# First weight quarter's blocks one slot earlier, values' turn behind the normalisation, fewer filling products

## Chip, cores and metric

The kernel runs on one core of one Trainium2 chip. The metric is the device time of one execution in microseconds (us); a lower time is better. Each time below is that of the one core.

## What is computed

Three layers follow each other on a batch of 4 sequences with 576 positions and 512 channels. The change lies in the first: attention of 8 heads of 64 channels with a decay, while the weights of the second layer are made ready beside it.

```
scores = (q @ k.T) / sqrt(64) + cum[i] - cum[j]      # cum = cumsum(log(clip(f)))
attn   = softmax(where(j > i, -1e9, scores));  x = attn @ v          # 32 heads
u      = x + (x.T @ U @ V).T;  y = u + relu(u @ w_ch1) @ w_ch2       # 512 -> 2048 -> 512
out    = top-2 gated mixture of 4 single-head attentions over y
```

## The kernel before

**Stages.** Attention of the 32 heads comes first, two heads (a pair) per 128 partitions. Then a dense stage works off the rest of the second layer, and the mixture ends the program. Products of the second layer (hidden groups L704 and output groups L720) already run between the heads from head 10 on; they need the first quarter of the weights (`w1h`, `w1l`, `w2h`, `w2l`).

**The order.** Within the head stage the program writes down events: `put(h, us, do)` places a step at `us` in slot h (8.4 nominal units per slot, L1026). The events are sorted by that number, and each engine, SP's DMA queue included, gets its instructions in that order and works them off in order. The numbers set the order alone; how long a slot takes is decided by the engines. A slot runs below from the first score product of head h (PE, L285) to that of the next.

**A head's way.** PE multiplies scores in two parts (L285, tile `sc`), ScalarE takes exponentials (L305, L1050), and splits them into a high part (L310) and DVE's remainder (L313, tile `ph`). In the next slot PE weights the values (L341 to L345, or L357 for the odd heads of the first five pairs, which use the plain 32-bit form in two pieces; tile `av`), and DVE makes denominators (`den`, L403 or L405), their reciprocals (L408) and the normalised output (L422). Two slots ahead of a head PE makes the products for its row maxima (`ua` L201, `ub` L219), DVE takes the maxima (L206, L227, tile `mx`), PE turns them (`mt` L233), ScalarE makes a row of them (`mr` L239), and SP moves it to its place (L243). The `sc`, `ua` and `ub` tiles share two buffers.

**Values' turn.** From the second pair on, the largest value of a pair is found in an even slot: DVE takes the maximum per partition (`am` L363), PE turns it (`amt` L368, `value_turn`), and `value_power` makes a power of two of it in three small DVE operations (L375 to L377). At the start of the next odd slot PE spreads it (`rsp` L383), right behind `mt` and ahead of the second score part.

**Blocks.** The first quarter of the weights comes in 8 blocks of 128 x 512, as 64-bit words: SP reads (`raw`, L457 or L460), ScalarE narrows in two operations (`low_bits`, L442 and L443), DVE joins in two (`join_bits`, L449 and L450), ScalarE copies the high part and DVE subtracts the remainder (the last lines of `weight_events`, L1318 and L1320). `raw` and the joined block have two buffers each. The second quarter's blocks pass through the same function later, in slots of even number.

**Ones.** `busy` lets PE multiply a tile of ones with itself, a few products of 128 columns, whose result nobody reads.

**Sums.** In odd slots PE also makes the sums of the pair before (`gp` L943, `up` L960 and L962), ScalarE and DVE their parts (`g` L947 and L950, `ustage` L967). GpSimd subtracts 64 x 576 pieces of the next pair's q and k (L932), and from head 10 on masks the exponentials (L1056).

The events that the change touches, in the code before:

```
        put(h, 4.54, step, "amt", "am", value_turn)
        put(h, 5.6, step, "full", "amt", value_power)
        put(h + 1, 0.57, step, "rp", "full", value_spread)
        ...
        put(h - 1, 2.9, read)
        put(h, 8.0 if h % 2 else 6.1, bits)
        put(h + 1, 2.0, lambda: join_bits(st["to"], pairs_of_words(st["raw"])))
```

Of the kernel before, what the change touches and what calls it, by code (L numbers as in the profile page):

```python
# [15 lines left out]
OP = mybir.AluOpType  # L16
# [15 lines left out]
FT = FF // P // NQ  # L32
# [46 lines left out]
def f32(ap):  # L79
    return ap.bitcast(F32)  # L80
# [3 lines left out]
def kernel(  # L84
# [13 lines left out]
    nc = tc.nc  # L98
# [262 lines left out]
    def value_max(vr):  # L361
        am = small.tile([P, 1], F32, name="am")
        nc.vector.tensor_reduce(am[:], vr, AX.XYZ, OP.max, apply_absolute_value=True)  # L363
        return am
# [21 lines left out]
    def value_factor(rp):  # L386
        rs = small.tile([P, 1], F32, name="rs")
        nc.vector.reciprocal(rs[:], rp[:])
        return rs

    def value_high(vr, rs, vh):
        nc.scalar.mul(vh[:, :, :, 0:64], vr, rs[:, 0:1])

    def value_low(vr, rs, vh, vl):
        nc.vector.scalar_tensor_tensor(vl[:], vr, rs[:, 0:1], vh[:, :, :, 0:64], OP.mult,
                                       OP.subtract)
# [41 lines left out]
    def low_bits(wt, raw):  # L438

        lo, hi = raw[:, :, 0], raw[:, :, 1]  # L440
        byte = raw.bitcast(U8)[:, :, 3]
        nc.scalar.activation(wt.bitcast(I32), byte, AF.Copy, bias=-31.0 / 64.0, scale=1.0 / 32.0)  # L442
        nc.scalar.activation(f32(lo), f32(hi), AF.Copy, scale=2.0 ** -112)  # L443

    def join_bits(wt, raw):

        lo, hi = raw[:, :, 0], raw[:, :, 1]
        wi = wt.bitcast(I32)
        nc.vector.scalar_tensor_tensor(wi, lo, 3, wi, OP.logical_shift_left, OP.bitwise_or)  # L449
        nc.vector.scalar_tensor_tensor(wi, hi, -2147483648, wi, OP.bitwise_and, OP.bitwise_or)  # L450

    def read_block(q, t, from_=None):

        c0 = (q * FT + t % FT) * P
        raw = (from_ or stage).tile([P, 2 * DM], I32, name="raw", tag="wraw")
        if t < FT:
            nc.sync.dma_start(raw[:].rearrange("p (k n) -> p k n", k=KT),  # L457
                              w1[:, 2 * c0:2 * c0 + 2 * P].rearrange("(k p) n -> p k n", p=P))
        else:
            nc.sync.dma_start(raw[:], w2[c0:c0 + P, :])  # L460
        return raw

    def pairs_of_words(raw):
        return raw[:].rearrange("p (n two) -> p n two", two=2)
# [273 lines left out]
    dense, casts, sums, jobs, deferred, late = [], [], {}, [], [], []  # L738
# [287 lines left out]
    def put(h, us, do, *what):  # L1026
        events.append((h * SLOT + us, len(events), do, what))

    def early(us, do, *what):
        put(0, us - FIRST, do, *what)  # L1030
# [94 lines left out]
    def value_events(p):  # L1125

        h = 2 * (p - 1)
        st = {}

        def step(name, of, do):  # L1130
            st[name] = do(st[of]) if of else do(places[p % 2][1])

        def factor():
            st_rs[p] = value_factor(st["rp"])

        vr = places[p % 2][1]
        vh, vl = vhs[p % 2]
        if p < NPLAIN:
            vr = vr[:, 0:1]
            vh, vl = firsts[p % 2]  # L1140
        elif p < NPLAIN + 2:
            put(h + 1, 6.0, lambda: nc.vector.memset(vh[:, :, :, 64:65], 1.0))
        if p == 0:
            early(6.6, step, "am", None, lambda _: value_max(vr))
            put(0, 0.3, step, "amt", "am", value_turn)
            put(0, 0.35, step, "full", "amt", value_power)
            put(0, 2.05, step, "rp", "full", value_spread)
            put(0, 2.1, factor)
            put(0, 4.95, lambda: value_high(vr, st_rs[p], vh))
            put(0, 8.0, lambda: value_low(vr, st_rs[p], vh, vl))  # L1150
            return
        put(h, 1.95, step, "am", None, lambda _: value_max(vr))
        put(h, 4.54, step, "amt", "am", value_turn)
        put(h, 5.6, step, "full", "amt", value_power)
        put(h + 1, 0.57, step, "rp", "full", value_spread)
        put(h + 1, 2.2, factor)
        put(h + 1, 6.1, lambda: value_high(vr, st_rs[p], vh))
        put(h + 2, 1.9, lambda: value_low(vr, st_rs[p], vh, vl))
# [132 lines left out]
    def weight_events(q, t, h):  # L1291

        w1h, w1l, w2h, w2l = W[0]
        st = {}

        def read():
            st["raw"] = read_block(q, t)

        def bits():
            if q == 0:  # L1300
                st["to"] = stage.tile([P, DM], F32, name="wst", tag="wst")[:]
            else:
                st["to"] = w32[q][:, t, :]
            low_bits(st["to"], pairs_of_words(st["raw"]))

        put(h - 1, 2.9, read)
        put(h, 8.0 if h % 2 else 6.1, bits)
        put(h + 1, 2.0, lambda: join_bits(st["to"], pairs_of_words(st["raw"])))
        if q:
            return  # L1310
        cs = slice(t * P, t * P + P)
        dh, dl = (w1h[:, :, cs], w1l[:, :, cs]) if t < FT else (w2h[:, t - FT, :],
                                                               w2l[:, t - FT, :])

        def view():
            return st["to"].rearrange("p (k n) -> p k n", k=KT) if t < FT else st["to"]

        put(h + 1, 6.7, lambda: nc.scalar.copy(dh, view()))  # L1318
        put(*((h + 2, 2.3) if t < 2 * FT - 1 else (h + 1, 8.38)),
            lambda: nc.vector.tensor_tensor(dl, view(), f32(dh), OP.subtract))  # L1320

    def largest_event(t, h):

        def largest_of():
            if t == 0:
                largest[1] = small.tile([P, 2, FT], F32, name="wam0", bufs=1)
            nc.vector.tensor_reduce(largest[1][:, t // FT, t % FT:t % FT + 1], w32[1][:, t, :],
                                    AX.X, OP.max, apply_absolute_value=True)

        put(h, 2.45, largest_of)  # L1330
# [26 lines left out]
        for _ in range(n):  # L1357
            nc.tensor.matmul(some[:, 0:P], every[:], every[:], start=True, stop=True)

    for h in range(10):  # L1360
        put(h, 0.54, busy, 8 if h < 3 else 4)
        if h < 3 or h % 2:
            put(h, 2.1, busy, 14 if h < 3 else 10)
    early(12.35, busy, 24)

    NHEAD = 2 * NPAIR
# [5 lines left out]
    for p in range(NPAIR):  # L1372
        value_events(p)
        split_events(p)
        mix_events(p)
        for n, (j, us, ta, td) in enumerate(((0, 2.1, 3.95, 5.45), (1, 2.1, 3.95, 5.45),
                                             (0, 5.9, 7.6, 8.2), (1, 7.1, 8.75, 10.3))):
            if n < PER_PAIR[p]:
                fill_events(2 * p + j, us, ta, td)
    for t in range(2 * FT):  # L1380
        weight_events(0, t, (4, 5, 6, 7, 8, 9, 10, 11)[t])
        weight_events(1, t, 2 * (t + 7))
        largest_event(t, (20, 22, 24, 26, 28, 29, 30, 31)[t])
    put(9, 8.35, ffn_prepare, 0)
# [745 lines left out]
```

## Time and profile before

| what | value |
|---|---|
| median of 3 runs (lowest to highest) | 786.92 us (786.47 to 787.28) |
| the profiled execution's own time | 787.25 us |
| its span, first to last instruction | 785.5 us |
| busy: PE, DVE, ACT, POOL | 752.3, 598.5, 436.1, 201.9 us |
| head stage (slots 0 to 31) | 16.8 to 266 us of the span |
| slots 3 to 9, mean of one | 7.34 us |
| slots 10 to 29, mean of one | 8.51 us |

The span is what the profile shows of that execution; the 1.7 us beside it lie before its first and behind its last instruction. In the profile, PE is TensorE's matmuls, PEld its weight loads, DVE VectorE, ACT ScalarE, POOL GpSimd, SPq the DMA queue of SyncE. L12 is line 12 of the kernel. Matmuls overlap each other, so their starts tell more than their durations. In brackets stands how long the engine was idle before an instruction, and what ended that wait.

### The profile page before, as it was taken

To read this page: it belongs to the slowest core of one execution; us is meant where nothing else is said; L and a number is where in the kernel's file an instruction comes from. 1 tells how busy PE (TensorE), PEld (TensorE's weight loads), DVE (VectorE), ACT (ScalarE), POOL (GpSimd) and SP (SyncE) were. 2 spreads that over 40 slices of the span, in tenths; PEclk is the share of its full clock that TensorE was granted. 3 is DMA by queue.
4 is the path that set the end of the run, shared out by engine and by line. 5 is a ranking of instruction groups with operands and counts; after the bars stand their busy time and mean duration, and the time that the engine had idled before them with its cause. 6 is when DMAs were issued, how large, how long until landed. Compare 5 with 4: busy or idle time off the path is not lost.

```text
span 785.5 us, 19296 instructions
## 1 busy us (share of the span) xinstructions
PE 752.3 (96%) x7399; PEld 649.0 (83%) x7399; DVE 598.5 (76%) x1659; ACT 436.1 (56%) x893; POOL 201.9 (26%) x357
## 2 busy tenths in 40 slices
PE   4899999999999999999999999999999999999996
PEld 4799888989998999877777777777778888878873
DVE  6889999999999959988773685366644688887763
ACT  6778887877786725644421242113312366776673
POOL 8734466665564200000020000000000611111110
PEclk9999999999999999999999999999999999999999
DMA  5668665566563165844133224300103475344322
GB/s 163 174 195 227 194 179 169 178 183 180 172 188 116 61 197 184 266 145 168 54 99 109 73 80 158 113 1 1 62 31 76 120 182 139 76 118 97 91 75 95
DMA packets 65708, 101.97 MB, mean 130 GB/s; under 512 B 8864, under 2 KB 43664, under 8 KB 65616
## 3 DMA queue, kind: packets, MB, share of 16 engines
q1 hardware_dynamic: 65248, 100.09, 43.0%
q8 instruction: 58, 0.95, 0.5%
q10 hardware_dynamic: 368, 0.66, 0.3%
q14 instruction: 34, 0.28, 0.1%
HBM read 53.25 MB, written 23.74 MB: 98 GB/s over the span
## 4 chain that ended last, share of the span: by engine, by line
PE 53%; DVE 2%; ACT 1%; issue 0%; DMA 0%; ACTq 0%; DVEq 0%
PE cps L720 17%; PE hps L704 16%; PE pq L1636 6%; PE pv L1680 3%; PE sc L285 3%; PE po L1732 2%; PE ub L219 1%; PE av L341 1%; PE av L345 1%; PE av L343 1%; PE pos L1732 1%; PE ua L201 0%; DVE ph L313 0%; ACT pf L305 0%; DMA out_dram<-ost 0%
## 5 line engine op out<-in xcount | busy, mean ns | idle before, releaser
L709 ACT ACTIVATE hh<-hps 128x288 f16<-128x288 f32 (+1 forms) x128 | 52.4, 410 | 210.6 <-PE hps L704 186.1
L710 DVE SCALAR_TENSOR_TENSOR hl<-hps,hh 128x288 f16<-128x288 f32 (+1 forms) x128 | 58.2, 454 | 79.5 <-ACT hh L709 79.1
L227 DVE CUSTOM_DVE_ANT_0 ub<-ub,maskm 128x448 f32<-128x448 f32 x192 | 82.4, 429 | 2.3 <-PE ub L219 0.7
L285 PE MATMUL sc<-qa,ka 128*128 128x288 f32 (+4 forms) x288 | 72.0, 309 | 1.6 <-DMA qa<-mr 1.1
L726 DVE SCALAR_TENSOR_TENSOR yc<-cps,back,yc 128x288 f32<-128x288 f32 x96 | 49.3, 514 | 24.5 <-PE cps L720 23.0
L285 PE MATMUL sc<-qb,kb 128*128 128x288 f32 (+4 forms) x288 | 63.5, 302 | 0.0
L341 PEld LDWEIGHTS <-ph 128*128 128x128 f16 x645 | 58.9, 97 | 1.2 <-DVE o L422 0.6
L345 PEld LDWEIGHTS <-ph 128*128 128x128 f16 x645 | 59.3, 97 | 0.4 <-DVE ph L313 0.4
L343 PEld LDWEIGHTS <-ph 128*128 128x128 f16 x645 | 59.3, 98 | 0.3
L1863 POOL TENSOR_SCALAR_AFFINE_SELECT pf<-pf 128x128 f32<-128x128 f32 (+1 forms) x80 | 23.9, 318 | 116.3 <-ACT pf L305 115.6
L285 PEld LDWEIGHTS sc<-qb,kb 128*128 128x128 f32 x288 | 52.3, 189 | 1.5
L206 DVE CUSTOM_DVE_ANT_0 ua<-ua,maskm 128x576 f32<-128x576 f32 x48 | 36.5, 761 | 21.0 <-PE ua L201 12.3
L313 DVE TENSOR_TENSOR ph<-pf,ph 128x512 f16<-128x512 f32 (+1 forms) x66 | 47.6, 734 | 6.4 <-ACT ph L310 6.4
L285 PEld LDWEIGHTS sc<-qa,ka 128*128 128x128 f32 x288 | 48.8, 189 | 3.7 <-issue 1.2
L313 DVE TENSOR_TENSOR ph<-aside,ph 128x512 f16<-128x512 f32 (+1 forms) x63 | 49.8, 802 | 1.2 <-ACT ph L310 1.0
L1056 POOL TENSOR_SCALAR_AFFINE_SELECT aside<-aside 128x128 f32<-128x128 f32 (+1 forms) x80 | 39.6, 514 | 38.5 <-ACT aside L305 29.9
L305 ACT ACTIVATE aside<-sc 128x512 f32<-128x512 f32 (+1 forms) x63 | 38.7, 617 | 18.3 <-PE sc L285 16.5
L720 PE MATMUL cps<-hh,w16b 128*128 128x288 f16 x256 | 48.3, 286 | 0.3 <-DVE hl L710 0.3
L720 PE MATMUL cps<-hh,w1lf 128*128 128x288 f16 x256 | 48.4, 286 | 0.0
L720 PE MATMUL cps<-hh,w16a 128*128 128x288 f16 x256 | 48.4, 286 | 0.0
L305 ACT ACTIVATE pf<-sc 128x512 f32<-128x512 f32 (+1 forms) x66 | 39.7, 609 | 13.1 <-PE sc L285 9.4
L720 PEld LDWEIGHTS <-w16b 128*128 128x128 f16 x384 | 37.4, 98 | 10.2 <-issue 0.8
(281 smaller groups left out, 2464.4 us busy)
## 6 DMA issues: line engine op xcount, KB each, us to landing
raw<-in_w_dram SPq DMA_DIRECT2D x32, 512.0 KB
ust<-udram SPq DMA_DIRECT2D x13, 576.0 KB
ydram<-yc SPq DMA_DIRECT2D x10, 576.0 KB
aside<-in_qk_dram SPq DMA_DIRECT2D x8, 576.0 KB
room<-in_qk_dram SPq DMA_DIRECT2D x8, 576.0 KB
udram<-ustage SPq DMA_DIRECT2D x16, 288.0 KB
ydram<-ust SPq DMA_DIRECT2D x8, 576.0 KB
yc<-ydram SPq DMA_DIRECT2D x8, 576.0 KB
```

The source lines that it names most:

```text
L227: nc.vector.tensor_tensor_reduce(ub[:, bk, off:off + w], ub[:, bk, off:off + w], maskm[:, S - w:S], 1.0, NEG, OP.add, OP.max, mx[:, t:t + 1])
L285: nc.tensor.matmul(ps[:, bk, off:off + w], wa, xa, start=bk not in banks[:n], stop=bk not in banks[n + 1:])
L305: nc.scalar.activation(pf[:, 0:S].rearrange("p (c n) -> p c n", c=2) if whole else pf[:, 0:n], view, AF.Exp, scale=ISC)
L313: nc.vector.tensor_tensor(pl[:, o0:o0 + n], pf[:, 0:n], ph[:, o0:o0 + n], OP.subtract)
L341: nc.tensor.matmul(av[:, it, :], ph[:, c:c + P], vh[:, jt, :], start=first, stop=False)
L343: nc.tensor.matmul(av[:, it, 0:64], ph[:, c:c + P], vl[:, jt, :], start=False, stop=False)
L345: nc.tensor.matmul(av[:, it, :], pl[:, c:c + P], vh[:, jt, :], start=False, stop=last)
L704: nc.tensor.matmul(ph[:], wa[:, k, fs], xa[:, k], start=n == 0, stop=n == 3 * KT - 1)
L709: after(lambda: nc.scalar.activation(hh[:], ph[:], AF.Relu), lambda: nc.vector.scalar_tensor_tensor(hl[:], ph[:], 0.0, high, OP.max, OP.su ...
L710: lambda: nc.vector.scalar_tensor_tensor(hl[:], ph[:], 0.0, high, OP.max, OP.subtract))
L720: nc.tensor.matmul(pc[:], wa[:, t, dsl], xa[:], start=n == 0, stop=n == 3 * FT - 1)
L726: nc.vector.scalar_tensor_tensor(yc[:, d, :], pc[:], back, yc[:, d, :], OP.mult, OP.add)
```

## The change

It edits numbers of the order, and leaves out products; nothing else of the computation is touched.

- The values' turn comes after the attention product, and `value_power` after the normalisation (all pairs from the second on).
- The eight blocks of the first quarter are taken one slot earlier. Those whose number of slot is odd (four of them) are narrowed behind the next slot's exponentials, joined behind its normalisation, and their high part is made in the slot after. Their reads but the first stand behind the moves of the even slot before. The last block's remainder takes the usual place.
- The ones from slot 3 on are left out: 4 products in each of slots 3 to 9, and 10 more in 3, 5, 7 and 9.

```diff
-        put(h, 4.54, step, "amt", "am", value_turn)
-        put(h, 5.6, step, "full", "amt", value_power)
+        put(h, 4.7, step, "amt", "am", value_turn)
+        put(h, 6.57, step, "full", "amt", value_power)
...
-        put(h - 1, 2.9, read)
-        put(h, 8.0 if h % 2 else 6.1, bits)
-        put(h + 1, 2.0, lambda: join_bits(st["to"], pairs_of_words(st["raw"])))
+        late = h % 2
+        put(h - 1, 6.65 if late and t else 2.9, read)
+        put(*((h + 1, 3.2) if late else (h, 6.1)), bits)
+        put(h + 1, 6.6 if late else 2.0,
+            lambda: join_bits(st["to"], pairs_of_words(st["raw"])))
...
-        put(h + 1, 6.7, lambda: nc.scalar.copy(dh, view()))
-        put(*((h + 2, 2.3) if t < 2 * FT - 1 else (h + 1, 8.38)),
-            lambda: nc.vector.tensor_tensor(dl, view(), f32(dh), OP.subtract))
+        put(*((h + 2, 1.4) if late else (h + 1, 6.7)), lambda: nc.scalar.copy(dh, view()))
+        put(h + 2, 2.3, lambda: nc.vector.tensor_tensor(dl, view(), f32(dh), OP.subtract))
...
-    for h in range(10):
-        put(h, 0.54, busy, 8 if h < 3 else 4)
-        if h < 3 or h % 2:
-            put(h, 2.1, busy, 14 if h < 3 else 10)
+    for h in range(3):
+        put(h, 0.54, busy, 8)
+        put(h, 2.1, busy, 14)
...
-        weight_events(0, t, (4, 5, 6, 7, 8, 9, 10, 11)[t])
+        weight_events(0, t, (3, 4, 5, 6, 7, 8, 9, 10)[t])
```

DVE at the end of slot 4, from the second of the row maxima (ISA with `ub`; the second ISA row of each reads the result) to the denominators. Before:

```order
L227 ISA ub,mx_96<-ub,maskm 128x448
L227 ISA mx_96 128x1
L375 TENSOR_REDUCE ar_82<-amt 1x1
L376 TENSOR_SCALAR ar_82<-ar_82 1x1
L377 TENSOR_SCALAR ar_82<-ar_82 1x1
L227 ISA ub,mx_96<-ub,maskm 128x320
L227 ISA mx_96 128x1
L403 TENSOR_SCALAR den<-av 128x5
```

And with the change, up to the same place:

```order
L227 ISA ub,mx_96<-ub,maskm 128x448
L227 ISA mx_96 128x1
L227 ISA ub,mx_96<-ub,maskm 128x320
L227 ISA mx_96 128x1
L403 TENSOR_SCALAR den<-av 128x5
```

The three operations on `ar` have left the row of maxima. DVE a little later, at the start of slot 5, from the normalisation to the next head's first maximum. Before:

```order
L422 TENSOR_TENSOR room<-av,rn 128x5x64
L313 TENSOR_TENSOR ph_144<-pf,ph_144 128x512
L313 TENSOR_TENSOR ph_144<-aside,ph_144 128x512
L449 SCALAR_TENSOR_TENSOR wst<-raw,wst 128x512
L450 SCALAR_TENSOR_TENSOR wst<-raw,wst 128x512
L388 RECIPROCAL rs<-rsp 128x1
L206 ISA ua,mx_90<-ua,maskm 128x2x288
```

With the change, from the normalisation to the remainder ahead of that maximum:

```order
L422 TENSOR_TENSOR room<-av,rn 128x5x64
L375 TENSOR_REDUCE ar_82<-amt 1x1
L376 TENSOR_SCALAR ar_82<-ar_82 1x1
L377 TENSOR_SCALAR ar_82<-ar_82 1x1
L449 SCALAR_TENSOR_TENSOR wst<-raw,wst 128x512
L450 SCALAR_TENSOR_TENSOR wst<-raw,wst 128x512
L313 TENSOR_TENSOR ph_144<-pf,ph_144 128x512
L313 TENSOR_TENSOR ph_144<-aside,ph_144 128x512
L449 SCALAR_TENSOR_TENSOR wst<-raw,wst 128x512
L450 SCALAR_TENSOR_TENSOR wst<-raw,wst 128x512
L388 RECIPROCAL rs<-rsp 128x1
L1321 TENSOR_TENSOR w1l<-wst,w1h 128x4x128
```

The three operations come behind the normalisation here, followed by a second join and, later, by a block's remainder. PE at the end of slot 4, as a difference, from the last products for the maxima to the next head's scores:

```order
 L219 MATMUL ub<-ka_128,qa_126 128x192
 L219 MATMUL ub<-ka_128,qa_126 128x64
+L357 MATMUL av<-vw_158,ph_146 128x65 x9
 L368 MATMUL amt<-ident,am 1x128
-L357 MATMUL av<-vw_158,ph_146 128x65 x9
 L285 MATMUL sc<-qa_138,ka_140 128x288
 L285 MATMUL sc<-qb_139,kb_141 128x288
```

The values' turn has moved from ahead of the attention product's second piece to behind it.

## Rows read from the trace of the kernel before

**Rows 1.** The page's slices of the span: PE's busy tenths, its granted clock.

```profile
PE   4899999999999999999999999999999999999996
PEclk9999999999999999999999999999999999999999
```

**Rows 2.** Slot 5: us; busy PE, PEld, DVE, ACT, POOL (xinstructions); clock, DMA, GB/s.

```profile
53.27:60.62 7.35, 7.31 (x104) 6.98 (x103) 6.50 (x22) 5.36 (x11) 3.42 (x4) 1.00 0.69 198
```

**Rows 3.** Timeline of DVE, slots 4 and 5: start us, us, engine line operation out<-in.

```profile
52.19 0.27 DVE L375 TENSOR_REDUCE ar<-amt 1x1 f32<-1x128 f32 x1
...
52.75 0.48 DVE L227 CUSTOM_DVE_ANT_0 ub<-ub,maskm 128x320 f32<-128x320 f32 x1
...
53.50 0.16 DVE L403 TENSOR_SCALAR den<-av 128x5 f32<-128x5 f32 x1 [0.22 <-PE av L357]
...
56.15 0.68 DVE L449 SCALAR_TENSOR_TENSOR wst<-raw,wst 128x512 int32<-128x512 int32 x1
...
57.47 0.16 DVE L388 RECIPROCAL rs<-rsp 128x1 f32<-128x1 f32 x1
...
58.14 0.77 DVE L206 CUSTOM_DVE_ANT_0 ua<-ua,maskm 128x576 f32<-128x576 f32 x1 [0.51 <-ACT g L947]
```

**Rows 4.** Timelines of PE and DVE, slots 6, 7, 10 and 11.

```profile
65.60 0.76 PE L219 MATMUL ub<-ka,qa 127*128 127x448 f32 x4 [0.94 <-ACT pf L305]
...
66.31 2.12 PE L357 MATMUL av<-vw,ph 128*128 128x65 f32 x18
...
68.47 0.17 DVE L403 TENSOR_SCALAR den<-av 128x5 f32<-128x5 f32 x1
...
68.92 0.39 PE L1358 MATMUL some<-every 128*128 128x128 bf16 x4
...
70.85 0.72 PE L1358 MATMUL some<-every 128*128 128x128 bf16 x10
...
97.02 2.12 PE L357 MATMUL av<-vw,ph 128*128 128x65 f32 x18
...
99.55 0.15 DVE L403 TENSOR_SCALAR den<-av 128x5 f32<-128x5 f32 x1
...
101.33 0.46 DVE L710 SCALAR_TENSOR_TENSOR hl<-hps,hh 128x288 fp32r<-128x288 f32 x1 [0.53 <-ACT hh L709]
```

**Rows 5.** Timelines of GpSimd and DVE, slots 7 and 10.

```profile
68.77 1.42 POOL L932 TENSOR_TENSOR kb<-room,ka 64x576 fp32r<-64x576 f32 x1
...
69.55 1.18 DVE L313 TENSOR_TENSOR ph<-aside,ph 128x512 f16<-128x512 f32 x1
...
94.93 0.69 DVE L450 SCALAR_TENSOR_TENSOR wst<-raw,wst 128x512 int32<-128x512 int32 x1
...
95.00 1.47 POOL L1056 TENSOR_SCALAR_AFFINE_SELECT pf<-pf 128x128 f32<-128x128 f32 x2
...
95.54 0.78 DVE L1320 TENSOR_TENSOR w2l<-wst,w2h 128x512 fp32r<-128x512 f32 x1
```

**Rows 6.** Timeline of DVE, slot 13.

```profile
119.77 0.68 DVE L1320 TENSOR_TENSOR w2l<-wst,w2h 128x512 fp32r<-128x512 f32 x1
...
120.37 0.68 DVE L313 TENSOR_TENSOR ph<-aside,ph 128x512 f16<-128x512 f32 x1
...
123.73 0.77 DVE L206 CUSTOM_DVE_ANT_0 ua<-ua,maskm 128x576 f32<-128x576 f32 x1 [1.06 <-PE ua L201]
```

**Rows 7.** Waits of DVE from 125 to 262 us; then the timeline of slot 17.

```profile
DVE ua L206 <- PE ua L201: 3.1, 7, 0.6
...
150.41 0.48 DVE L422 TENSOR_TENSOR room<-av,rn 128x320 f32<-128x320 f32 x1
...
150.60 0.08 PEld L233 LDWEIGHTS mt<-ident,mx 128*5 128x5 f32 x1 [0.34 <-DVE mx L227]
...
150.71 0.17 PE L383 MATMUL rsp<-ar,every 128*128 128x1 bf16 x1
...
155.11 0.77 DVE L206 CUSTOM_DVE_ANT_0 ua<-ua,maskm 128x576 f32<-128x576 f32 x1 [0.48 <-PE ua L201]
```

## Prediction

> **What bounds the kernel now.** I read the page's slices first: PE is the busy engine nearly everywhere, and its granted clock is at full speed in every slice, also in the first, where PE works less than half of the time [rows 1]. The change touches the stretch of 32 attention heads, from 17 to 266 us, one slot per head. So I then cut that stretch into slots (a slot runs from the first score product of a head to that of the next) and read the busy time by slot, the waits, and the order of time on each engine. In slot 5 DVE works 6.50 of 7.35 us [rows 2]; from slot 6 to 12 it pauses nearly nowhere, and the waits that I found in slots 5 to 13 are short: 0.22 us for a finished attention product before its denominators and 0.51 before the first maximum in slot 5 [rows 3], 0.53 for a hidden part in slot 11 [rows 4], 1.06 before the first maximum in slot 13 [rows 6]. So DVE sets the pace of slots 5 to 12, in step with PE: once in each slot DVE needs PE's products for the maxima (ua) and once or twice PE waits for DVE. Later, in the odd slots, a short chain is what ends last: DVE's last maximum, PE's turn of the maxima (mt), the spread of the value factor (rsp), the second score products, a hidden or output group, the sums (gp), ua, and DVE again. DVE waits for ua in 7 slots of that stretch, 3.1 us in all [rows 7].
>
> **Values' turn behind the normalisation.** The three small operations of value_power take 0.56 us from start to start (52.19 to 52.75, where the next maximum starts) [rows 3]. They now stand behind the last maximum and the normalisation. So mt may start 0.56 us sooner, but rsp comes right behind mt on PE and needs the third of the three, and the second score products queue behind rsp. Maxima and normalisation move up by 0.56 and the three take the place behind them, so that they end where the normalisation ended. In slot 17 that is 150.41 + 0.48 = 150.89; with 0.04 from one engine to the next (68.43 to 68.47, worked out below), rsp starts at 150.93 instead of 150.71 [rows 7]: 0.22 us later. There DVE already waits 0.48 us for ua, and that wait grows. This holds in the odd slots in which PE waits for the maxima before mt: 13, 15, 17, 19, 23, 27 and 29, while in 21 and 25 PE comes late by itself. The term is 7 x 0.22 = **+1.5 us**. Its ends: nothing, if something that I don't see takes up the 0.22, and 7 x 0.56 = 3.9.
>
> In slots 3, 5, 7 and 9 the delay is larger, about 0.7 us, since DVE there waits for the attention product before it can go on (0.22 us in slot 5 [rows 3]), and the three operations no longer fill that wait. But there the 14 ones go from PE's odd slots, 4 of them ahead of mt and 10 ahead of gp; four take 0.39 and ten 0.72 us [rows 4], so each holds PE for 0.33 / 6 = 0.055, the four for 0.22 and the ten for 0.55, and the second pays for most of the delay. All 68 of them (4 in each of seven slots, 10 in four) are worth nothing beyond that, as PE then only waits longer for DVE's maxima.
>
> **Blocks one slot up.** A block costs DVE a join (two operations, 56.15 to 57.47 where the next one starts, so 1.32 us [rows 3]) and a remainder (119.77 to 120.37, where the 0.68 of the row are overlapped by the next, so 0.60 [rows 6]). The sum over all eight blocks stays. What moves is one block's 1.92 us, out of slots 12 and 13 and into slot 5 (the join of the first block is put at the end of slot 4 and done at the start of slot 5). In slot 5 it fills the wait of 0.51 us; at the end only the join's 1.32 comes back, because the last remainder (119.77) lies in front of the 1.06 us for which DVE waits anyway [rows 6]. So 1.92 - 0.51 - 1.32 = **+0.1 us**.
>
> **Joins in pairs.** The blocks of odd slots are now joined behind the normalisation, so DVE has two joins in each of slots 5, 7, 9 and 11, and none in 6, 8 and 10. In an even slot DVE thus reaches the denominators 1.32 + 0.56 = 1.88 us sooner. It then waits for PE, which reaches the end of the attention product sooner by less: in slot 6 by 0.94, the wait of ub for ScalarE's exponentials that the later narrowing removes, 0.22 for the ones and 0.11 for the values' turn that now stands behind the product. In the profile both arrive together (66.31 + 2.12 = 68.43 and 68.47 [rows 4]), so at the start of slot 7 DVE newly waits 1.88 - 1.27 = 0.6. Slots 8 and 9 have the same pattern: 0.6. In slot 4 nothing of this is gained except the 0.56 that no longer fills the wait, less 0.11: 0.45. In slot 10 PE has a hidden group and no ones, and gains the 0.11 alone; DVE came 0.41 after the product (97.02 + 2.12 = 99.14 and 99.55 [rows 4]), so it waits 1.88 - 0.41 - 0.11 = 1.36, of which the 0.53 that it now waits for the hidden part is to be taken off, since the join covers that: 0.85. Together 0.45 + 0.6 + 0.6 + 0.85 = **+2.5 us**; the ends are 0 (PE runs ahead enough) and 3.0 (the join covers nothing). In the following odd slots the time isn't won back, since there DVE, with two joins, is the one that PE waits for.
>
> **Beside GpSimd.** The first remainder of the exponentials takes 1.18 us in slot 7 while GpSimd's subtraction runs (68.77 to 70.19), and 0.68 alone [rows 5, 6]. The first now comes 2 us later, behind the first join, when that subtraction has ended: up to -0.5 in each of slots 5, 7 and 9; I take -0.4, because the subtraction comes later too and may still reach into it. In its place the join stands beside GpSimd, and a weight's remainder beside GpSimd's next subtraction. The nearest rows, beside its selection: a join's second half takes its usual 0.69, a weight's remainder 0.78 instead of 0.68 [rows 5, 6]. By these: -1.2 + 3 x 0.1 = **-0.9 us**, with ends of -1.5 and +1.5. The Trainium skill's GPSIMD Engine Reference (section 8, Key points) speaks against that: GpSimd shares its SBUF interfaces with VectorE, and contends with instructions that have two SBUF inputs. The join has two such inputs; by that rule it would stretch as the remainder did, and this term would be 0 and the time 0.9 us longer. The rows show no join beside a GpSimd subtraction, so the run will tell.
>
> **Other edits.** Narrowing behind the exponentials and the high part behind its join cost ScalarE the same work as before; ScalarE isn't what paces these slots, so 0. The reads of the odd slots' blocks move past the moves on SP's queue, and each now waits there for a join that DVE does early in the next slot, with the next row of maxima (qa<-mr) queued behind it. That row is needed at the start of the slot after. DVE's join stands in the first half of its slot, so the row leaves before the slot ends: 0. If it came late in slots 6, 8 and 10, PE would wait by what is missing, a few tenths each.
>
> **Sum.** +1.5 + 0.1 + 2.5 - 0.9 = +3.2 us on the profiled execution's 787.25 us, so 790.45. That execution lies 0.33 above the median of 786.92; against the median I forecast 786.92 + 3.2 = **790.1 us**, slower by 0.4%.
>
> **Rivals.** (1) *PE runs ahead, faster.* If the exponentials' 0.94 and the ones bring the attention product to its end before DVE asks for it, the paired joins cost nothing, and what DVE waited goes: 0.51 and 0.22 in slot 5, 0.53 in slot 11 and, with a join less in slot 12 and PE no longer late, 0.66 of slot 13's 1.06. That is 1.9 off the median: 785.0. For it speaks that PE is gated by ScalarE in slots 6, 8 and 12; against it, that PE gains 1.27 where DVE gains 1.88. It decides at a wait before the denominators in slots 7 and 9 under 0.1 us. (2) *The two halves partly cancel.* The paired joins cost half as much and the late chain half, 1.25 + 0.75 - 0.9 + 0.1 = 1.2: 788.1, within what can be told from no change. (3) *TensorE's clock falls.* Without the ones PE pauses longer from slot 3 on. The clock stayed full in a slice with PE busy under a half [rows 1], so I hold this unlikely; if one slot ran at 1.2 GHz, its 7.31 us of PE work [rows 2] would take twice as long, 786.92 + 3.2 + 7.3: 797. The Trainium skill (TensorE: Matmul & The Clock Gate, Part 1) says that the throttled clock is the default and activity releases it, which is what the ones would serve; no row here shows the clock at the lower level.
>
> **Chances.** Forecast 0.58, rival 1 0.18, rival 2 0.20, rival 3 0.04. About 0.2%, 1.57 us, is what can be told from no change. Rival 1 is the faster case, 0.18; rival 2 the same, with 0.04 of the forecast's own low end: 0.24; slower 0.58. The forecast's own range is 788.5 to 791.9; with the greater part of rival 1, the range for 8 in 10 is 785.0 to 791.9.
>
> **What would show it.** Right: in slots 7 and 9 DVE's den waits some 0.6 us for av; two joins stand in slots 5, 7, 9 and 11; rsp waits for ar and the wait of DVE for ua in slots 15, 17, 19, 23 and 27 is about 0.7 instead of 0.5; slot 16 starts about 2 us later than before. Wrong: no wait at den, slot 14 starts no later than before, or the granted clock below 1.00 in a slice.

## The result and the profile after

The changed kernel takes 797.46 us (median of 4 runs, 795.54 to 799.49) where the kernel before takes 787.10 beside it: 1.0124 times as long, 95% interval 1.0105 to 1.0142, or 10.4 us slower. The forecast was 790.1 us and its range ended at 791.9. Run a second time it took 795.63 us (4 runs, 794.91 to 796.68), 1.0107 times before (1.0090 to 1.0124). The profiled execution took 798.38 us, its span 796.7 against 785.5.

By the starts of the slots, the profiled execution is 3.15 us behind before at slot 4, 8.0 at slot 13 and 10.3 at slot 30. The second run's profile, which lacks the first loss, is 0.2 us ahead at slot 4, 4.7 behind at slot 13 and 8.6 at slot 30. Slot 27 is 2.43 us longer there and 0.86 in the first profile, so 1.6 of the last belong to a stretch at the lower clock (0.5 from 245.7 to 249.1 us). Behind the head stage both profiles lose another 0.8 us, at 303 us of the kernel before: PE waits there 0.4 and 0.6 us for the factor of another spread (L490). No part alone shows this loss.

PE's share and its granted clock in 40 slices of the changed kernel's page, which answer to [rows 1]:

```profile
PE   4797899999999999999999999999999999999997
PEclk9899999999999999999999999999999999999999
```

The second slice is below full speed. In windows: us; busy PE, PEld, DVE, ACT, POOL (xinstructions); clock, DMA, GB/s. The first and second are the stretches at half the clock (1.2 GHz), the third and fourth are slots 5 and 6:

```profile
23.27:26.69 3.42, 3.34 (x18) 3.10 (x19) 3.25 (x13) 3.25 (x8) 3.27 (x3) 0.50 0.82 194
...
33.51:36.93 3.42, 3.42 (x20) 3.23 (x20) 2.21 (x5) 2.31 (x5) 0.24 (x1) 0.50 0.05 12
56.38:66.57 10.19, 7.32 (x90) 6.22 (x89) 9.79 (x29) 7.06 (x16) 5.95 (x4) 1.00 0.58 184
66.57:72.84 6.27, 6.27 (x56) 6.16 (x56) 5.72 (x18) 6.21 (x14) 0.15 (x1) 1.00 0.82 211
```

Slot 5 has grown from 7.35 [rows 2] to 10.19 us, slot 6 has shrunk from 7.62 to 6.27. DVE is busy for 9.79 of the 10.19. Slots 7 and 9 are like slot 5, slot 8 like slot 6. The timeline of slot 5 (start, us, engine, line; in brackets the wait and what ended it), and then of slot 17, which answers to [rows 7]:

```profile
56.55 0.17 DVE L403 TENSOR_SCALAR den<-av 128x5 f32<-128x5 f32 x1 [0.65 <-PE av L357]
...
58.07 1.42 POOL L932 TENSOR_TENSOR kb<-aside,ka 64x576 fp32r<-64x576 f32 x1
...
58.22 1.82 DVE L449 SCALAR_TENSOR_TENSOR wst<-raw,wst 128x512 int32<-128x512 int32 x1
60.08 0.69 DVE L450 SCALAR_TENSOR_TENSOR wst<-raw,wst 128x512 int32<-128x512 int32 x1
...
60.80 0.62 ACT L1320 CAST w1h<-wst 128x512 fp32r<-128x512 f32 x1 [1.77 <-DVE wst L450]
...
62.46 0.76 PE L219 MATMUL ub<-ka,qa 127*128 127x448 f32 x4 [1.21 <-ACT ph L1050]
...
63.30 0.67 DVE L1321 TENSOR_TENSOR w1l<-wst,w1h 128x512 fp32r<-128x512 f32 x1
63.37 1.87 POOL L932 TENSOR_TENSOR qb<-aside,qb 64x576 fp32r<-64x576 f32 x1 [3.88 <-ACT qb L886]
63.88 0.76 DVE L206 CUSTOM_DVE_ANT_0 ua<-ua,maskm 128x576 f32<-128x576 f32 x1
...
156.88 0.13 DVE L227 DVE_READ_ACCUMULATOR2_ANT mx<- 128x1 f32 x1
157.05 0.50 DVE L227 CUSTOM_DVE_ANT_0 ub<-ub,maskm 128x320 f32<-128x320 f32 x1
157.46 0.22 DVE L405 TENSOR_SCALAR den<-av,rs 128x5 f32<-128x5 f32 x1
...
158.47 0.27 PE L233 MATMUL mt<-ident,mx 128*5 128x128 f32 x1
158.65 0.27 DVE L375 TENSOR_REDUCE ar<-amt 1x1 f32<-1x128 f32 x1
159.13 0.14 DVE L377 TENSOR_SCALAR ar<-ar 1x1 int32<-1x1 int32 x1
159.32 0.16 PE L383 MATMUL rsp<-ar,every 128*128 128x1 bf16 x1 [0.58 <-DVE ar L377]
...
163.74 0.77 DVE L206 CUSTOM_DVE_ANT_0 ua<-ua,maskm 128x576 f32<-128x576 f32 x1 [0.75 <-PE ua L201]
```

Two things stand out. The first half of the join (L449) takes 1.82 us beside GpSimd's subtraction, not 0.68 [rows 3], and all that follows on DVE comes later; ScalarE's high part waits 1.77 us for it ahead of the exponentials, and PE's ub 1.21 us for these. And rsp waits 0.58 us for ar, where it came 0.11 behind mt before [rows 7]. Waits from 36 to 265 us, from within slot 2 to slot 29 (us in total, times, longest; the 2.7 of the first row stands in slot 2):

```profile
DVE ua L206 <- PE ua L201: 9.6, 11, 2.7
...
PE rsp L383 <- DVE ar L377: 6.6, 11, 0.6
...
DVE den L403 <- PE av L357: 2.1, 5, 0.6
```

The wait of rsp stands in 11 odd slots; that of DVE for the denominators in slots 3, 5, 7, 9 and 10.

### The profile page after: what moved, and what is told of

The parts are those of the page before. It is cut to its first block, busy times and chain, and to the rows that moved or that the text cites. A ratio compares the mean times of both kernels' runs of the same rounds, so it can differ in the third digit from the quotient of the medians.

```text
span 796.7 us, 19157 instructions
## 1 busy us (share of the span) xinstructions
PE 753.7 (95%) x7331; PEld 648.3 (81%) x7331; DVE 601.9 (76%) x1659; ACT 436.7 (55%) x893; POOL 199.3 (25%) x357
## 4 chain that ended last, share of the span: by engine, by line
PE 50%; DVE 3%; ACT 1%; DMA 1%; issue 0%; SPq 0%; ACTq 0%; DVEq 0%
PE cps L720 16%; PE hps L704 15%; PE pq L1636 6%; PE pv L1680 3%; PE sc L285 3%; PE po L1732 2%; PE ub L219 1%; PE av L341 1%; PE av L345 1%; PE av L343 1%; DMA ust<-udram 1%; PE pos L1732 1%; PE ua L201 0%; DVE ph L313 0%; DVE uam L576 0%
## 5 line engine op out<-in xcount | busy, mean ns | idle before, releaser
L206 DVE CUSTOM_DVE_ANT_0 ua<-ua,maskm 128x576 f32<-128x576 f32 x48 | 36.5, 761 | 24.4 <-PE ua L201 16.2
L313 DVE TENSOR_TENSOR ph<-pf,ph 128x512 f16<-128x512 f32 (+1 forms) x66 | 47.2, 728 | 6.4 <-ACT ph L310 6.4
L313 DVE TENSOR_TENSOR ph<-aside,ph 128x512 f16<-128x512 f32 (+1 forms) x63 | 47.3, 761 | 2.6 <-ACT ph L310 2.6
L1056 POOL TENSOR_SCALAR_AFFINE_SELECT aside<-aside 128x128 f32<-128x128 f32 (+1 forms) x80 | 37.3, 484 | 41.6 <-ACT aside L305 35.6
```

Of the source, the lines that this page charges most:

```text
L313: nc.vector.tensor_tensor(pl[:, o0:o0 + n], pf[:, 0:n], ph[:, o0:o0 + n], OP.subtract)
```

## Experiments

Each is compared with runs of the kernel before on the same chip, whose medians were 786.79 to 787.19 us.

### The three parts, each alone

**The turn.**

```diff
-        put(h, 4.54, step, "amt", "am", value_turn)
-        put(h, 5.6, step, "full", "amt", value_power)
+        put(h, 4.7, step, "amt", "am", value_turn)
+        put(h, 6.57, step, "full", "amt", value_power)
```

> The kernel before with the values' turn alone: amt behind the attention product, value_power behind the normalisation. Theory A (the three parts add up, and this one costs what the late odd slots show): in the trace of the changed kernel the denominators of slot 17 come 0.39 us sooner against the maxima, but rsp starts 1.86 us behind the denominators' start where it started 1.08 behind them before, so 0.39 us later in each of 7 late odd slots, and some 0.4 to 0.7 in slots 3, 5, 7 and 9: +2.7 + 2 = +4.5 us. Rival B (the turn costs little by itself, since in slots 3 to 9 the joins and not rsp end last): +2 us or less. If the turn is what brings TensorE's clock to its lower level in slots 1 and 2 as in the changed kernel's profile, this run shows it and a slot 3 that starts 3 us late; if not, slot 3 starts at most 0.3 us late.

Measured: 793.16 us, 1.0076 (1.0064 to 1.0088), +6.0. The profiled execution (792.34) loses 0.73, 0.71, 0.60 and 0.59 in slots 3, 5, 7 and 9, 2.6 together, and 2.95 from slot 13 to 30. Slot 1 ran at half the clock here too, yet slot 2 started no later. So A in kind: the median lies 1.5 us above its 4.5, the profiled execution 0.6. The loss before slot 4 is not the turn's.

**The ones.**

```diff
-    for h in range(10):
-        put(h, 0.54, busy, 8 if h < 3 else 4)
...
+    for h in range(3):
+        put(h, 0.54, busy, 8)
```

> The kernel before with the ones from slot 3 on left out, and nothing else. Theory A (the ones fill PE's pauses and cost nothing there; the clock stays full without them): within 0.5 us of before, -0.5 to +0.5, the granted clock 1.00 in all slices. Rival B (they keep the clock at full speed, or they hold PE up): B1, without them the clock falls in a stretch between slot 3 and 10, +2 us or more; B2, they hold up mt and gp, and the time falls by up to 7 x 0.22 + 4 x 0.55 = 3.7 us.

Measured: 786.66 us, 1.0000 (0.9989 to 1.0012). In the mean nothing, as A said, but both rivals hold in part, and they cancel. Slots 3 and 5 are 0.55 us shorter each, and slot 8 begins 1.37 us ahead of before. Then this profile shows the clock at half, from about 80 to past 86 us (same columns as the windows above), and slot 8 takes 9.55 instead of 7.63 us:

```profile
75.00:78.00 3.00, 3.00 (x29) 2.90 (x27) 2.89 (x7) 2.96 (x7) 0.00 (x0) 1.00 0.97 236
78.00:80.00 2.00, 0.93 (x6) 0.69 (x6) 1.97 (x4) 2.00 (x5) 0.00 (x0) 0.96 0.34 71
80.00:82.00 2.00, 2.00 (x12) 2.00 (x12) 1.93 (x9) 2.00 (x4) 0.99 (x1) 0.50 0.92 363
```

PE was busy for 0.93 of the 2 us ahead of it. Of 12 executions, four had a mean clock of 0.989 to 0.994 and took 788.0 to 789.8 us; the other eight had 0.996 or more and took 785.6 to 786.9. The 23 executions of before beside them all had 0.996 or more. The ones do not hold the clock in every execution, though: beside the other experiments 3 of 52 executions of before had 0.993 or 0.994, and two runs below that keep the ones have 0.988 or less throughout.

**The blocks.**

```diff
-        put(h, 8.0 if h % 2 else 6.1, bits)
-        put(h + 1, 2.0, lambda: join_bits(st["to"], pairs_of_words(st["raw"])))
+        put(*((h + 1, 3.2) if late else (h, 6.1)), bits)
+        put(h + 1, 6.6 if late else 2.0,
+            lambda: join_bits(st["to"], pairs_of_words(st["raw"])))
...
-        weight_events(0, t, (4, 5, 6, 7, 8, 9, 10, 11)[t])
+        weight_events(0, t, (3, 4, 5, 6, 7, 8, 9, 10)[t])
```

> The kernel before with the blocks alone: one slot up, the odd ones narrowed behind the exponentials and joined behind the normalisation. Theory A (the joins that now stand beside GpSimd's subtraction are stretched from 0.68 to 1.8 us, and the high parts wait for them ahead of the exponentials, so that ub and up wait): slots 4 to 13 take 3 to 5 us longer, +4 us in all, and the wait of PE for ACT's high part (ph L1050) of 1.2 us stands in slots 5, 7 and 9. Rival B (in the changed kernel the late rsp of the values' turn was what made these slots long): +1.5 us or less, though the stretched joins are there.

Measured: 791.25 us, 1.0049 (1.0037 to 1.0061), +4.1. All of it stands between slots 5 and 14, and it stays at 4.2 from there to slot 30. A's size is right; PE's wait for the exponentials is 0.9 us in each of slots 5, 7 and 9, not 1.2. DVE and GpSimd in slot 5:

```profile
54.98 1.74 POOL L932 TENSOR_TENSOR kb<-aside,ka 64x576 fp32r<-64x576 f32 x1
...
55.48 1.78 DVE L450 SCALAR_TENSOR_TENSOR wst<-raw,wst 128x512 int32<-128x512 int32 x1
```

At the start of slot 6 PE waits another 0.98 us for the row of maxima (`qa<-mr`). On SP's queue its move stands behind the read of a block, which waits for this join. The prediction named that path under "Other edits" and put it at nothing. In the changed kernel PE does not wait there.

The parts add up to 6.0 - 0.5 + 4.1 = 9.6 us, against 10.4 and 8.6 for the whole in its two runs.

### Why the turn costs 6 us

The turn alone, and the spread behind the second score products:

```diff
-        put(h + 1, 0.57, step, "rp", "full", value_spread)
+        put(h + 1, 0.65, step, "rp", "full", value_spread)
```

> The kernel before with the values' turn as in the changed kernel, but the spread (rsp) put behind the second score products, which then need not wait for ar. Theory A (the turn costs because rsp stands ahead of the second score products on PE): the wait for ar falls from 0.6 us to nothing, as the score products take about that long, and the time is within 0.8 us of before, or up to 1 us below it. Rival B (the turn costs for another reason, such as DVE's three operations ahead of the next head's remainders): as long as the run with the turn alone, +2 to +4.5 us.

Measured: 786.49 us, 0.9991 (0.9982 to 1.0000). The 6.0 us are gone, 0.7 beside. In slot 17 rsp comes with no wait, as the second score products run while DVE makes ar:

```profile
150.60 0.27 PE L233 MATMUL mt<-ident,mx 128*5 128x128 f32 x1 [0.20 <-DVE mx L227]
150.63 0.71 PE L285 MATMUL sc<-qa,ka 128*128 128x320 f32 x3
...
151.78 0.18 PE L383 MATMUL rsp<-ar,every 128*128 128x1 bf16 x1
```

So the whole price of the turn lies in rsp's place on PE's queue.

### Why the blocks cost 4 us

**The shift alone**: the last line of the blocks' diff, with the old rules.

> The kernel before with the eight blocks one slot earlier and nothing else: the old rules of narrowing and joining, one join in each slot from 4 to 11. Theory A (my prediction's term for the shift): slot 5 longer by 1.4 us, slots 12 and 13 shorter by 1.3, +0.1 us in all, within 0.6 us of before. Rival B (the shift itself costs, since the first join meets GpSimd's subtractions or the reads disturb the rows in slots 3 and 4): +1 us or more.

Measured: 786.91 us against 786.79, 0.9997 (0.9985 to 1.0008). Slot 4 is 1.20 us longer, slots 12 and 13 are 0.39 and 0.86 shorter: the 0.1 of the forecast within the noise, in slot 4 because the old rules join the first block there.

**GpSimd's part taken out**, with the blocks and then without them:

```diff
+            if j == 0 and p in (4, 5, 6):
+                dst, src, high = dst[:, :32], src[:, :32], high[:, :32]
             nc.gpsimd.tensor_tensor(dst, src, f32(high), OP.subtract)
```

> The blocks alone, and GpSimd's subtractions beside slots 5, 7 and 9 (first head of pairs 4 to 6) cut from 576 to 32 columns: the other 544 columns of those low parts are left out. Theory A (the contention with GpSimd is the larger part of what the blocks cost): no join takes over 0.85 us any more, slots 5, 7 and 9 become about 1 us shorter each, and the time falls by 2.5 to 3.3 us, to about 1 us above before. Rival B (the joins in pairs cost by their place, stretched or not, as my prediction had it with 2.5 us): it falls by 1 us or less.

> The kernel before with the same cut of GpSimd's subtractions (544 of 576 columns left out for the first head of pairs 4 to 6), so that the cut with the blocks can be read. Theory A: a remainder is no longer stretched, 3 x 0.5 us less for DVE in slots 5, 7 and 9, of which slot 5 gives nothing, as DVE waits 0.51 us there: -0.7 to -1.2 us. Rival B (DVE's time there is worth nothing, or PE sets the pace): 0 to -0.3 us.

Measured: with the blocks 786.65 us, 0.9990 (0.9981 to 0.9999), 4.6 below the blocks alone and more than A expected. Without them 787.08, 0.9997 (0.9985 to 1.0008): nothing, rival B. Slot 5 with the blocks and the cut:

```profile
53.60 0.25 POOL L934 TENSOR_TENSOR qb<-aside,qa 64x32 fp32r<-64x32 f32 x1 [5.58 <-ACT qa L883]
54.17 0.24 POOL L934 TENSOR_TENSOR kb<-aside,ka 64x32 fp32r<-64x32 f32 x1 [0.33 <-ACT ka L884]
...
54.73 0.68 DVE L449 SCALAR_TENSOR_TENSOR wst<-raw,wst 128x512 int32<-128x512 int32 x1
55.45 0.69 DVE L450 SCALAR_TENSOR_TENSOR wst<-raw,wst 128x512 int32<-128x512 int32 x1
```

So the meeting with GpSimd is the whole price of the blocks. That GpSimd itself ends later is not it: with the blocks alone, no wait from 45 to 131 us ends with one of its subtractions. Without the meeting the joins in pairs cost nothing: 786.65 against 787.08 is 0.4 less, not 2.5 more. The odd slots 5 to 11 are 0.8 to 1.2 us longer, and slots 6, 8, 10, 12 and 13 together win that back.

**Other places for the high part and the join.** Two runs meant to tell the high part's wait from the join's stretch:

```diff
-        put(*((h + 2, 1.4) if late else (h + 1, 6.7)), lambda: nc.scalar.copy(dh, view()))
-        put(h + 2, 2.3, lambda: nc.vector.tensor_tensor(dl, view(), f32(dh), OP.subtract))
+        put(*((h + 2, 3.0) if late else (h + 1, 6.7)), lambda: nc.scalar.copy(dh, view()))
+        put(h + 2, 4.5 if late else 2.3, lambda: nc.vector.tensor_tensor(dl, view(), f32(dh), OP.subtract))
```

> The blocks alone (4.1 us above before), with one edit: the odd blocks' high part on ScalarE stands behind the next slot's exponentials instead of ahead of them, and the remainder later in that slot. Theory A (DVE, with two joins of which one is stretched beside GpSimd, is what paces slots 5, 7 and 9; ScalarE's wait for the join is its consequence): the wait of ub for ScalarE goes, the time falls by 0.5 us at most. Rival B (the high part that waits for the join ahead of the exponentials is the bound, PE waits 0.9 us for it in slots 5, 7 and 9): the time falls by 2 us or more, to within 2 us of before.

Measured: 802.80 us, 1.0193 (1.0173 to 1.0214): 11.6 us longer than the blocks alone, against both expectations. ScalarE, which no longer waits, gives GpSimd its next operands sooner, and those subtractions now meet the second join and the remainder too. DVE and GpSimd in slot 5:

```profile
54.75 1.75 POOL L932 TENSOR_TENSOR kb<-aside,ka 64x576 fp32r<-64x576 f32 x1
...
55.26 1.79 DVE L450 SCALAR_TENSOR_TENSOR wst<-raw,wst 128x512 int32<-128x512 int32 x1
...
58.69 1.43 POOL L932 TENSOR_TENSOR qb<-aside,qb 64x576 fp32r<-64x576 f32 x1 [2.19 <-ACT qb L886]
58.89 1.78 DVE L450 SCALAR_TENSOR_TENSOR wst<-raw,wst 128x512 int32<-128x512 int32 x1
60.19 1.74 POOL L932 TENSOR_TENSOR kb<-aside,khigh 64x576 fp32r<-64x576 f32 x1
...
60.67 1.81 DVE L1321 TENSOR_TENSOR w1l<-wst,w1h 128x512 fp32r<-128x512 f32 x1
```

Three operations lose 1.1 us each, where the blocks alone had one. The mean clock fell to 0.986 as well, with three stretches at half the clock (20.5 us in all) in the profile. Slots 6 and 8 lie in part in these: PE is busy there without a pause, GpSimd does next to nothing, and they are 2.2 and 2.0 us longer than with the blocks alone. So at least some 4 of the 11.6 us are the clock's; the odd slots, which have both, do not divide. Then, on top of that edit, the odd joins behind the remainders of the exponentials:

```diff
-        put(h + 1, 6.6 if late else 2.0,
+        put(h + 1, 9.7 if late else 2.0,
```

> The blocks alone with the high part later as in the run before, and the odd blocks' joins put behind the two remainders of the exponentials, so that these stand beside GpSimd again, as in the kernel before. Theory A (a join is stretched by 1.1 us beside GpSimd, a remainder by 0.5): the joins take 0.68 again, a remainder 1.2, and the time falls by 3 x 0.6 = 1.8 us against the run with the later high part. Rival B (whatever stands beside GpSimd loses the same): no change within 0.5 us.

Measured: 800.09 us, 1.0161 (1.0135 to 1.0187), 2.7 us less. The total does not tell A from B, since this profile has 17 us at half the clock (from 63.7 us) where the run before had other stretches; the rows do. The joins take 0.68 again, as A said, but a remainder loses as much as a join did, not 0.5:

```profile
54.70 0.83 DVE L313 TENSOR_TENSOR ph<-pf,ph 128x512 f16<-128x512 f32 x1
55.46 1.90 DVE L313 TENSOR_TENSOR ph<-aside,ph 128x512 f16<-128x512 f32 x1
57.28 0.68 DVE L449 SCALAR_TENSOR_TENSOR wst<-raw,wst 128x512 int32<-128x512 int32 x1
```

So it does not matter whether DVE joins or subtracts; what sets the price is worked out below.

### The whole again

**The changed kernel with the late spread** (the one line above).

> The whole changed kernel with the spread (rsp) put behind the second score products. Theory A (the parts add up; what the turn costs is all in rsp's place): 797.5 less the 6.7 us by which the same edit moved the turn alone (793.2 to 786.5), so 790.8, 3.6 us above before. Rival B (in the changed kernel slots 5 to 13 are held by the stretched joins anyway, and the spread matters only in the later odd slots): 2 to 3 us come back, 794.5 to 795.5.

Measured: 791.47 us, 1.0049 (1.0033 to 1.0064), 4.7 above before: near A. Seven of the 9 executions had a clock of 0.991 to 0.995; the two at 0.999 took 789.53 and 789.88, about 3 us above before. In the profile of the first of these, slots 5 to 13 lose 3.9 us, near the blocks' 4.1, and slot 3 is 0.66 shorter without its ones.

**The changed kernel once more.**

> The changed kernel itself, unedited, once more. Its first profile had two stretches at the lower clock in slots 1 and 2 and a row of maxima (qa<-mr) that PE waited 2.33 us for, in all 3.15 us up to slot 4, in slots where the change has moved almost nothing. Theory A (that loss belongs to that execution and not to the change; the change itself costs the turn's 6.0 and the blocks' 4.1 less what the ones give): in an execution with the clock at 0.998 or above slot 4 starts within 0.7 us of before, and the time is 795 to 796 us; executions at a lower clock are longer. Rival B (the moved turn makes the row of slot 2 late each time): the wait of over 2 us is there again, and no execution is below 795.

Measured: 795.63 us; the executions at a clock of 0.998 and 0.999 took 794.91 and 795.01, those at 0.996 took 796.25 and 796.68. Slot 4 starts 0.18 us earlier than before. Waits of PE up to slot 3, of the first profile and then of this one:

```profile
PE sc L285 <- DMA qa<-mr: 3.2, 3, 2.3
```

```profile
PE sc L285 <- DMA qa<-mr: 0.8, 2, 0.5
```

A: the late row and the two stretches at half the clock belong to that execution.

**A version below both.** The turn, the late spread, and the 10 ones left out in slots 3 and 5 alone:

```diff
-        if h < 3 or h % 2:
+        if h < 3 or h in (7, 9):
```

> The turn with the late spread, and the 10 ones left out in slots 3 and 5 alone, where the run with fewer ones won 0.55 us each before its clock fell in slot 8; the others stay. Theory A: 786.5 - 1.1 = 785.4 us, 0.2% below before, with the granted clock full from slot 3 on. Rival B (fewer ones let the clock fall, or the late spread has won that time already): no better than 786.5.

Measured: 784.94 us, 0.9979 (0.9964 to 0.9993), 1.85 us below before: A. One of its 12 executions had a clock of 0.991 and took 788.82, the others 784.42 to 786.52.

## Why the prediction was wrong

| term | forecast | measured | by |
|---|---|---|---|
| turn, odd slots from 13 | +1.5 | +2.95 | the turn alone, slots 13 to 30 |
| turn in slots 3 to 9, less the ones | 0 | +2.6 less 1.1 | the turn and the ones alone |
| blocks one slot up | +0.1 | +0.1 | the shift alone |
| joins in pairs | +2.5 | none (0.4 less) | blocks and before, both with the cut |
| beside GpSimd | -0.9 | +4.6 | the blocks without and with the cut |

Together the parts measure +8.7 us, where +3.2 was forecast. The executions of the changed kernel at a clock of 0.998 or 0.999 took 794.91 to 796.55, 7.8 to 9.5 above before.

**Beside GpSimd** is the step that failed, in sign and size. It priced a join by the nearest rows of a join, 0.69 and 0.78 us beside GpSimd's selection [rows 5], and counted L313's relief as a gain. The rows of before tell the rule, read differently: L313 starts at 69.55 and ends at 70.73, 0.54 behind the subtraction's end at 68.77 + 1.42 = 70.19. In slots 4 to 11 of before, of both runs of the changed kernel and of the three runs of the blocks without the cut, every such DVE operation (joins, remainders) that starts within a subtraction ends 0.55 us behind it (one 0.58): L449 here at 58.22 + 1.82 = 60.04, the subtraction at 59.49. So the loss is what is left of GpSimd's operation less 0.13, for joins and remainders alike: 1.27 - 0.13 = 1.14 here, 0.5 in [rows 5]. DVE's operations that take an input from PSUM, maxima and normalisations, lose nothing in these runs: the maximum L206 starts at 63.88 within a subtraction that ends at 65.24, and takes its usual 0.76. Where DVE starts first, GpSimd waits: 1.87 us for the subtraction at 63.37, 0.07 behind L1321, which keeps its 0.67. The selections hold joins and remainders up in the same way (one that starts with more than 0.1 us of a selection left ends 0.54 to 0.61 behind it; the one exception starts at 94.21 in the kernel before, 0.03 behind a selection, and takes its 0.68). But each lasts 0.9 us at most and they take turns with DVE's operations, so that little is left of one when DVE starts: 0.23 for the remainder of 0.78 us in [rows 5], hence its 0.1. A short partner was taken as the price of a long one.

The Trainium skill (SBUF — State Buffer, section "SBUF: two separate sides") states this as a lock: of a DVE operation with two SBUF inputs and a GpSimd operation, whichever starts first holds the shared ports for the whole instruction, and the other blocks. The traces agree: joins and remainders (both inputs in SBUF) end 0.55 us behind the subtraction, and L206 beside one is not held up. The sentence that the prediction cited from the Trainium skill's GPSIMD Engine Reference (section 8, Key points) was right too, and was set aside for those rows; worked out as a stretch of 0.5 us, as the prediction did, it gave 0 where +4.6 was measured. The lock is inferred from when operations end; no run isolates the ports themselves.

The other half, L313's relief, was worth nothing: the cut in the kernel before, which gives the same relief, won 0.0 us.

**Joins in pairs.** Its 2.5 us do not appear once the subtraction is out of the way, so that part of rival 1 holds: the paired joins cost nothing. That "the time isn't won back" failed; the slots without a join win it back. The den wait that it built on is there in kind (0.65 in slot 5, 0.53 in slot 7), but the turn makes it: with the blocks alone it is 0.22 us at most.

**The turn.** The mechanism was right: rsp waits for ar and the second score products queue behind it; DVE's wait for ua in slot 17 grew from 0.48 to 0.75. The size was not. "Maxima and normalisation move up by 0.56" failed. Slot 17 before:

```profile
148.67 0.14 DVE L227 DVE_READ_ACCUMULATOR2_ANT mx<- 128x1 f32 x1
148.67 0.28 DVE L375 TENSOR_REDUCE ar<-amt 1x1 f32<-1x128 f32 x1
...
149.23 0.48 DVE L227 CUSTOM_DVE_ANT_0 ub<-ub,maskm 128x320 f32<-128x320 f32 x1
...
149.63 0.21 DVE L405 TENSOR_SCALAR den<-av,rs 128x5 f32<-128x5 f32 x1
```

From the start of the denominators to that of rsp it is now 159.32 - 157.46 = 1.86 us, before it was 150.71 - 149.63 = 1.08, so 0.78 more; and the denominators come only 0.39 sooner, because between the read of the second maximum and the next there are now 0.17 us (156.88 to 157.05) that the first of the three operations used to fill: 0.56 - 0.17 = 0.39. Left are 0.39 a slot, not 0.22, and 7 x 0.39 = 2.7. In slots 3 to 9 the delay of 0.7 was right (0.59 to 0.73), but the ones paid for it only in slots 3 and 5.

**The ones and the clock.** "Worth nothing beyond that" held for the mean alone. Without them more executions lose the full clock for a stretch, so that rival 3, held unlikely at 0.04, is part of the spread: the changed kernel's executions run from 794.91 us at 0.998 to 799.49 at 0.992. That its 797 lies beside the measured 797.46 is chance, since at 0.998 and above the loss is still 7.8 us or more. It was held unlikely for a wrong reading: the clock record of the kernel before begins at 15.8 us of the span, and the page counts what lies ahead of it as full. The ones that run from 13.9 us say otherwise:

```profile
13.86 2.44 PE L1358 MATMUL some<-every 128*128 128x128 bf16 x24
```

That is 0.1 us for each of the 24, where each further one cost 0.055 in [rows 4], so most of them ran at the lower level. In the rest of that slice, from 15.8 us on, PE is busy for 3.37 of 3.84 us, so no row shows the clock staying full through a long pause. What decides in which execution the clock falls stays open: slot 1 was at half the clock for a stretch also in profiles of the turn alone and of the shift alone, which keep the ones, at no cost to the start of slot 2, and the changed kernel's second profile has its stretch in slot 27, where neither kernel has ones.

Right was the shift. The edits to the narrowing were not tried alone; with GpSimd's part taken out they cost nothing together with the joins. Of the signs named, two joins did stand in the odd slots, rsp waited for ar, and DVE's wait for ua in slots 15, 17, 19, 23 and 27 was 0.74 to 0.78, near the 0.7 named; the wait for den was 0.53 and 0.22 in slots 7 and 9, not 0.6. None of these showed the step that failed. "Slot 16 starts about 2 us later" did: it came out at 8.2 in the first profile and 5.0 in the second.

## What to carry to other kernels

Before a DVE operation with two SBUF inputs is moved, look up which GpSimd operation runs where it lands and how long that one still has to go; that remainder is the price on DVE, and rows beside a shorter GpSimd operation do not give it. What queues behind it can add to that, as SP's row of maxima did. A step that waits for late data goes behind independent work on its in-order engine: one line that put rsp behind the second score products was worth 6.7 us with the turn alone, and 4.2 to 6.0 in the whole (5.1 to 6.0 between executions at a clock of 0.999). Products that nobody reads may hold the clock; judge their removal by many executions and their clocks, not by one profile.

## What the runs showed of the hardware

- DVE's joins and remainders (128x512, both inputs in SBUF) and GpSimd's subtractions take turns here: if DVE's starts second, it ends 0.55 us behind the subtraction, and takes up to 1.93 us instead of 0.68. If the subtraction starts second, it takes up to 1.87 us instead of 1.42. DVE's maxima and normalisations, which read PSUM, keep their times (0.76 and 0.48 us) within a subtraction.
- Freeing ScalarE can lengthen DVE: with the high part out of its way, GpSimd's operands came sooner and three DVE operations per odd slot took 1.8 us instead of one.
- The granted clock fell to half behind a pause of PE (0.93 us busy of 2, at 78 us in the run without ones), for a stretch in which slot 8 took 1.9 us longer; with half the clock for 3.4 us of slot 1, the turn alone lost nothing there (7.75 us, before 7.79), as PE had pauses to fill: it was busy for 7.59 us of that slot, before for 6.38.
